# Top-32 attention and a GELU block on one core: item 0's softmax ahead of item 3's score copies, and dummies ahead of the third pair's keys

## The chip, the cores and the metric

The kernel runs on one core of a Trainium2 chip. The metric is the device time of one execution in microseconds (us). Six names are used as the profile has them: PE is TensorE (matmuls; PEld is its load of the stationary operand), DVE is VectorE, ACT is ScalarE, POOL is GpSimd, SP is SyncE, which here only issues DMAs. Every engine works through its own queue in the order in which the kernel issued the instructions; an instruction that waits holds up all that stand behind it on the same engine. "L371" is line 371 of the kernel.

## The reference

Attention over 8 batches of 8 heads, 576 positions, head size 64, in which every query keeps only its 32 largest scores; its output, laid out as 4608 tokens of 512 numbers, goes through two matrix products with an exact GELU between them. All in float32.

```python
scores = scale * np.matmul(q, k.transpose(0, 1, 3, 2))
kth = np.partition(scores, -top_k, axis=-1)[..., -top_k:-top_k + 1]
scores = np.where(scores >= kth, scores, -1000000000.0)
attn = np.exp(scores - np.max(scores, axis=-1, keepdims=True))
attn = attn / (np.sum(attn, axis=-1, keepdims=True) + 1e-09)
x = np.matmul(attn, v)   # then as (4608, 512)
h = x @ w_in
out = (0.5 * h * (1.0 + erf(h / sqrt(2)))) @ w_out
```

## The kernel before

**Items and slots.** Two heads form a pair. An item is a block of 128 queries of one pair (or the last 64 queries of two pairs), and there are 144 of them. The program is one loop over slots (`for n in range(ahead)`), and each slot holds steps of several items, written out by hand: the scores of item n+2 (`scores`), the top 32 of item n (`top_k`), the softmax of item n-1 (`select`, `softmax`), the transposes of the softmax of item n-2 (`transposes`), the product with the values for item n-3 (`attend`). From slot 10 (`START`) on, PE's remaining room goes to the two products of the GELU block (`mlp`); before that there are no tokens for it yet.

**What one item costs on each engine.** PE makes the scores: the last keys into a small PSUM tile `t_ps` (L334) and the first 512 keys of both heads into `s_ps` (L371). ACT copies them to the tile `s` in SBUF (L342 and L379; item 0's first block has a DVE copy at L339). DVE finds the 32 largest (`larger` L407, MAX8 L466, MATCH_REPLACE8 L469) with POOL helping (`sum_up` L432, `smaller` L440). POOL then makes two numbers for each row, `neg` (L480) and `bias` (L481), in `threshold`. ACT makes the softmax of each head in place in two passes: `select` pushes the scores under the threshold far down (L500), `softmax` takes the exponential and its sum `den` (L512). POOL adds 1e-9 to `den` (L493), DVE takes the reciprocal `rden` (L487), and for the first items POOL turns it into a diagonal matrix `diag` (L526), which PE uses in the transposes (L556, L590). The reciprocal of item n-1 is issued at the end of the top 32 of item n (`last`, which is `inverse(n - 1)`), so DVE waits there for ACT's softmax of item n-1.

**Keys and queries.** PE transposes the keys and queries of a pair when they have come in (L282), in three pieces: the keys, the tails of both, the queries. ACT copies each piece out of PSUM (L287). Pair 2, the third pair, has its first piece in slot 0 and the other two in slot 1 (`first`), and items 4 and 5 need them.

**Weights.** In each slot ACT takes a piece of the GELU block's weights through three passes (`weights_size`, L206, L212, L213), and POOL adds the result up (`weights_add`, L228). They are loaded by SP (L189).

**Dummies.** `keep_busy(count, m)` issues matmuls whose result nobody reads, into a PSUM tile of their own (`warm`, L1040). Each dummy shows as two records in the trace. Slots 0 to 9 each have some.

**The order around the change.** In slot 0 ACT has the copies of item 2's scores, three passes over weights and the copy of the third pair's keys. In slot 1 ACT has, in this order: the copies of item 3's scores, select and softmax of item 0, the two copies of the third pair's other pieces, three passes over weights. PE in slot 0 has the scores of item 2, the transposes of the third pair's keys, 4 dummies; in slot 1 the scores of item 3, the other transposes of the third pair, 20 dummies.

Of the kernel before, what the change touches and what calls it, by code (L numbers as in the profile page):

```python
# [14 lines left out]
def kernel(  # L15
# [51 lines left out]
    ident = const.tile([P, P], f32, name="ident")  # L67
# [80 lines left out]
    START = 2 * NP + 2  # L148
# [46 lines left out]
    def parts(u):  # L195

        t, dst = words[u], weights_of(u)[3].bitcast(i32)
        return t[:, :, 0::2], t.bitcast(mybir.dt.int16)[:, :, 2::4], t[:, :, 1::2], dst

    def weights_size(u):  # L200


        if u not in words:
            return
        w, first, below, d = parts(u)
        nc.scalar.activation(below, first, func=AF.Prelu, bias=high, scale=2.0**-40, alpha=2.0**40)  # L206
        if on_dve(u):
            nc.vector.tensor_scalar(
                w.bitcast(i32), w.bitcast(u32), 2.0**-13, None, op0=ALU.mult
            )  # L210
        else:
            nc.scalar.activation(w.bitcast(i32), w.bitcast(u32), func=AF.Copy, scale=2.0**-13)  # L212
        nc.scalar.activation(d, below, func=AF.Prelu, bias=low, scale=2.0**59, alpha=2.0**-40)  # L213

    def on_dve(u):

        return SLOT_OF[u] in ON_DVE

    def waits(u):

        return u == ORDER[-1]
# [3 lines left out]
    def weights_add(u):  # L225
        if u in words:
            w, _, _, d = parts(u)
            nc.gpsimd.tensor_tensor(d, d, w.bitcast(i32), op=ALU.add)  # L228
        made.add(u)
# [80 lines left out]
    def row(i, e):  # L310
        return S_of[i][:, e * S : (e + 1) * S]
# [14 lines left out]
    def pair_tile(name, tag="pr"):  # L326
        return ps.tile([P, 2, 512], f32, tag=tag, bufs=1, name=name)
# [76 lines left out]
    def larger(i):  # L404

        if paired(i):
            nc.vector.tensor_tensor(lists_of[i][:, :, 0], *halves_of(i), op=ALU.max)  # L407
# [28 lines left out]
    def smaller(i):  # L436

        if paired(i):
            both, top = lists_of[i][:, :, 1].bitcast(i32), lists_of[i][:, :, 0].bitcast(i32)
            nc.gpsimd.tensor_tensor(into_of(i)[:, :, 1].bitcast(i32), both, top, op=ALU.subtract)  # L440
# [42 lines left out]
    def inverse(i):  # L483
        if i < 0 or i >= N:
            return
        st = stat_of[i]
        nc.vector.reciprocal(st["rden"], st["den"])  # L487

    def add_small(i):
        if i < 0 or i >= N:  # L490
            return
        st = stat_of[i]
        nc.gpsimd.tensor_scalar(st["den"], st["den"], 1e-9, None, op0=ALU.add)  # L493

    def select(i, e):

        if i < 0 or i >= N:
            return
        st, s = stat_of[i], row(i, e)
        nc.scalar.activation(s, s, func=AF.Prelu, bias=st["neg"][:, e : e + 1], scale=1.0, alpha=STEEP)  # L500
        selected.add((i, e))
# [3 lines left out]
    def softmax(i, e):  # L505

        if i < 0 or i >= N:
            return
        st, s = stat_of[i], row(i, e)
        if (i, e) not in selected:  # L510
            select(i, e)
        nc.scalar.activation(  # L512
            s, s, func=AF.Exp, bias=st["bias"][:, e : e + 1], scale=1.0,
            accum_out=st["den"][:, e : e + 1],
        )
# [99 lines left out]
    def closes(i):  # L615

        if not few[0] or i < 0 or i >= N:
            return False
        pair, t = items[i]
        return t < NM and t % 2 == 1 and pair % NP == NP - 1  # L620

    def copy_x():
        while copies:
            copies.pop()()
# [353 lines left out]
    def run_gelus():  # L978
        while waiting:
            gelus(waiting.pop(0))  # L980
            if eager[0]:
                run_small(9)

    def run_small(room):

        while summing:
            sums(summing.pop(0))
            room -= 4
        while small and room > 0:
            n, f = small.pop(0)  # L990
            f()
            room -= n
# [11 lines left out]
    def mlp(n):  # L1004
        for _ in range(n):
            if done[0] >= len(pieces) or pieces[done[0]][0] > ready[0] or left[0] == 0:
                return
            pieces[done[0]][1]()
            done[0] += 1
            left[0] -= 1  # L1010
            if eager[0]:
                run_gelus()
                run_small(9)
# [4 lines left out]
    def room_in(n):  # L1018

        x = n - START - 1  # L1020
        if x < 1:
            return 4
        if x >= len(sizes):
            return 0
        return sizes[x] + (1 if x % 2 == 0 else -1)
# [11 lines left out]
    def keep_busy(count, m):  # L1037
        warm = pair_tile("warm", "l1")
        for _ in range(count):
            nc.tensor.matmul(warm[:, 0, 0:P], lhsT=m, rhs=m, start=True, stop=True)  # L1040
# [40 lines left out]
    for n in range(ahead):  # L1081

        left[0] = room_in(n)
        few[0] = n > START + 2
        eager[0] = n > N
        left[0] += closes(n - 3) - closes(n - 2)
        if not waits(unit_in(n)):
            weights_add(unit_in(n))
        if n > 0:
            larger(n + 1)  # L1090
        for piece in squares_in.pop(n, []):
            piece()
        two = few[0] and n % 2 == 0 and n + 3 < N and items[n + 3][1] < NM
        scores(n + 2, two)
        if two:
            scores(n + 3)
        product = attend(n - 3)
        late = n > START
        if n < START:

            for e in range(2):
                select(n - 1, e)
            softmax(n - 1, 0)
        copy_x()
        if n == START:

            for e in range(2):
                select(n - 1, e)
            softmax(n - 1, 0)
        if waits(unit_in(n)):  # L1110
            weights_size(unit_in(n))
            weights_add(unit_in(n))
        mlp(1)
        if closes(n - 3):
            ready[0] = n_tok[0]
        if few[0] and n % 2:
            run_gelus()
        tr = transposes(n - 2)
        if product and n > START and done[0] < len(pieces) and pieces[done[0]][0] > ready[0]:

            for piece in tr[:1]:
                piece(n + 2 if few[0] else None)
            tr, ready[0] = tr[1:], n_tok[0]
        if not few[0] and n > START:
            softmax(n - 1, 0)
        mlp(1)
        if not late:
            softmax(n - 1, 1)
        if few[0]:
            softmax(n - 1, 0)  # L1130
            if n % 2:
                mlp(ODD)
        mlp(1)
        prep = prep_in.pop(n, [])
        if n == 0:
            weights_size(unit_in(1))
        if n == START + 1:

            for piece in prep:
                piece(None)  # L1140
            prep = []
        if len(prep) > 1 and len(tr) == 3:
            tr, prep = tr[:1] + prep[:1] + tr[1:], prep[1:]
        now = tr[:-1]
        if few[0]:
            now, tr, prep = tr + prep[:1], [], prep[1:]
        for x, piece in enumerate(now):
            piece(n + 2 if few[0] else None)
            ready[0] = n_tok[0]
            if few[0] and x == 2:  # L1150
                break
            mlp(1)
        ready[0] = n_tok[0]
        if late:
            softmax(n - 1, 1)
        if n > 0:
            smaller(n + 1)
        add_small(n - 1)
        for piece in tr[-1:] + prep:
            piece(None)  # L1160
            mlp(1)
        if n < START:

            keep_busy(4 if n == 0 else 8 if product else 20 if n == 1 else 14 if n < 5 else 18, ident)

        run_gelus()
        mlp(left[0])
        run_gelus()
        if n < N:
            top_k(n, lambda: inverse(n - 1))  # L1170
            if n == 0:
                larger(1)
        else:
            inverse(n - 1)
        threshold(n)
        if n == 0:
            smaller(1)
        normalise(n - 1)
        sum_up(n + 2)
        if n in sums_in:  # L1180
            weight_sums(sums_in[n])
        run_small(6)

        if n > 0 and not waits(unit_in(n + 1)):
            weights_size(unit_in(n + 1))
        for m in (n + 1, n + 2):

            if m > 2 and waits(unit_in(m)) == (m == n + 1):
                load_weights(m)
        if n < NP:  # L1190
            load("v", n)
        if n == 5:
            load("q", SQUARES)
            load("k", SQUARES)
# [38 lines left out]
```

## Time and profile before

| | |
|---|---|
| median of 3 runs | 1526.88 us (1526.75 to 1527.65) |
| the profiled execution, own time | 1526.42 us |
| its span in the trace | 1524.5 us |
| PE busy in the span | 1507.2 us |
| DVE busy | 1235.8 us |
| ACT busy | 1156.2 us |
| POOL busy | 1137.7 us |
| granted TensorE clock, mean | 0.997 of full speed |

The execution's own time is 1.92 us above the span, which runs from the first to the last instruction that the trace holds. In a timeline row the first number is the start, the second the time from the start of the row's first instruction to the end of its last, then engine, line, operation, output and inputs, shape and count; brackets give the idle time before it and what ended that. The busy time of PE includes the dummies.

### The profile page before, as it was taken

Reading aid. Unit: us, or ns where it says so; the run is one execution under the profiler, and the core shown is the slowest. Engines: PE = TensorE matmul, PEld = TensorE weight load, DVE = VectorE, ACT = ScalarE, POOL = GpSimd, SP = SyncE. Lnnn points to the kernel's source line nnn. Section 1 sums busy time; section 2 is a strip of 40 time slices with the busy share of each in tenths; the row PEclk is TensorE's granted clock in tenths of the full one; section 3 lists DMA queues with packets and bytes.
Section 4 is the critical chain, followed back from the end, with each engine's and each line's share of the span. In section 5 each row is a group of like instructions: output and inputs, shape, how many; then the busy total and the mean of one; then the engine's idle time right before and its main releaser. Section 6 shows DMA issues by size and latency. Waiting matters only on the chain.

```text
span 1524.5 us, 26920 instructions
## 1 busy us (share of the span) xinstructions
PE 1507.2 (99%) x9233; PEld 1191.5 (78%) x9233; DVE 1235.8 (81%) x3270; ACT 1156.2 (76%) x2038; POOL 1137.7 (75%) x1291
## 2 busy tenths in 40 slices
PE   7999999999999999999999999999999999999999
PEld 5776677877877778888887778887787777888887
DVE  7999899988888878788888887888888887887701
ACT  6999877877778787877777778787777878787730
POOL 6777567867888868777798878786788886877742
PEclk9999999999999999999999999999999999999999
DMA  6524310111101110012201111011110111000000
GB/s 179 152 83 122 80 45 1 27 35 32 24 21 26 40 38 15 1 30 47 40 15 24 28 27 46 1 27 35 32 25 22 24 31 32 15 1 15 8 14 14
DMA packets 195016, 56.27 MB, mean 37 GB/s; under 512 B 185888, under 2 KB 186432, under 8 KB 194880
## 3 DMA queue, kind: packets, MB, share of 16 engines
q1 hardware_dynamic: 193616, 54.14, 15.1%
q8 instruction: 72, 1.18, 0.3%
q14 instruction: 64, 0.52, 0.1%
q10 hardware_dynamic: 1200, 0.39, 0.1%
q0 software_dynamic: 64, 0.03, 0.0%
HBM read 45.08 MB, written 9.44 MB: 36 GB/s over the span
## 4 chain that ended last, share of the span: by engine, by line
PE 93%; ACT 0%; DVE 0%; issue 0%; POOL 0%; DVEq 0%
PE h_ps L712 34%; PE y_ps L856 20%; PE o L654 9%; PE tp L592 8%; PE s_ps L371 7%; PE seven L854 3%; PE y_ps L818 2%; PE y_ps L800 2%; PE y_ps L821 2%; PE tp_t L334 2%; PE o L665 1%; PE s_ps L386 1%; PE tp_t L562 1%; PE tp_t L348 0%; PE warm L1040 0%; PE tp L590 0%
## 5 line engine op out<-in xcount | busy, mean ns | idle before, releaser
L712 PE MATMUL h_ps<-xT,w_in_sb 128*128 128x256 f32 (+1 forms) x2560 | 544.0, 361 | 0.1
L712 PEld LDWEIGHTS h_ps<-xT,w_in_sb 128*128 128x128 f32 x2560 | 433.7, 191 | 71.0 <-issue 25.2
L466 DVE MAX8 top<-lists 128x8 f32<-128x576 f32 (+1 forms) x792 | 477.0, 641 | 0.1
L469 DVE MATCH_REPLACE8 lists<-top,lists 128x288 f32<-128x288 f32 (+1 forms) x528 | 307.3, 587 | 0.0
L535 POOL TENSOR_TENSOR s<-s,rden 128x1152 f32<-128x1152 f32 x135 | 286.0, 2119 | 0.3 <-DVE rden L487 0.3
L493 POOL TENSOR_SCALAR den<-den 128x2 f32<-128x2 f32 x144 | 31.6, 219 | 284.5 <-ACT s L512 282.8
L512 ACT ACTIVATE s<-s,bias 128x576 f32<-128x576 f32 x288 | 224.8, 784 | 10.7
L500 ACT ACTIVATE s<-s,neg 128x576 f32<-128x576 f32 x288 | 225.8, 792 | 0.0
L606 ACT COPY pt<-tp 128x1024 f32<-128x1024 f32 x133 | 135.2, 1017 | 110.8 <-PE tp L592 110.8
L487 DVE RECIPROCAL rden<-den 128x2 f32<-128x2 f32 x144 | 23.8, 165 | 213.8 <-POOL den L493 213.3
L440 POOL TENSOR_TENSOR lists<-lists 128x576 int32<-128x576 int32 x132 | 186.4, 1412 | 4.0
L432 POOL TENSOR_TENSOR lists<-s 128x576 int32<-128x576 int32 x133 | 187.3, 1408 | 0.0
L654 PEld LDWEIGHTS o<-pt,raw_v 128*64 128x64 f32 x1280 | 87.1, 136 | 85.2 <-issue 44.3
L654 PE MATMUL o<-pt,raw_v 128*64 128x256 f32 x1280 | 153.0, 384 | 0.7 <-ACT pt L597 0.4
L856 PE MATMUL y_ps<-w_out_sb,sum 128*128 128x256 f32 x472 | 140.4, 379 | 0.0
L592 PE MATMUL tp<-ident,s 128*128 128x128 f32 x1080 | 140.1, 273 | 0.0
L592 PEld LDWEIGHTS tp<-ident,s 128*128 128x128 f32 x1080 | 126.4, 141 | 14.5 <-issue 1.9
L379 ACT ACTIVATE s<-s_ps 128x1024 f32<-128x1024 f32 x127 | 125.2, 1032 | 11.3 <-PE s_ps L371 11.2
L371 PE MATMUL s_ps<-kt,qm 64*128 64x512 f32 x512 | 130.3, 622 | 0.8 <-ACT s L377 0.8
L469 DVE MATCH_REPLACE8 lists<-first,lists 128x288 f32<-128x288 f32 x264 | 114.1, 437 | 0.0
L856 PE MATMUL y_ps<-w_out_sb,g 128*128 128x256 f32 x480 | 113.4, 379 | 0.0
L728 ACT ACTIVATE g<-h_ps 128x512 f32<-128x512 f32 x144 | 78.2, 595 | 42.1 <-PE h_ps L712 41.4
(163 smaller groups left out, 2515.1 us busy)
## 6 DMA issues: line engine op xcount, KB each, us to landing
raw_v<-in_v_dram SPq DMA_DIRECT2D x64, 128.0 KB, 2.3
out_dram<-y SPq DMA_DIRECT2D x30, 256.0 KB, 2.0
raw_q<-in_q_dram SPq DMA_DIRECT2D x112, 64.0 KB, 2.0
raw_k<-in_k_dram SPq DMA_DIRECT2D x112, 64.0 KB, 2.0
w_out_sb<-in_moe_w_in_dram SPq DMA_DIRECT2D x14, 511.8 KB, 4.7
w_out_sb<-in_moe_w_out_dram SPq DMA_DIRECT2D x10, 511.8 KB, 4.3
w_sum<-in_moe_w_out_dram SPq DMA_DIRECT2D x6, 511.8 KB, 4.3
raw_q<-in_q_dram SPq DMA_DIRECT2D x112, 8.0 KB, 1.8
```

The lines of the kernel that those rows point to most:

```text
L371: nc.tensor.matmul(s_ps[:, e], lhsT=q_t[rows, :], rhs=kt[rows, 0:SM], start=True, stop=True)
L432: nc.gpsimd.tensor_tensor(t[:, :, 1].bitcast(i32), a.bitcast(i32), b.bitcast(i32), op=ALU.add)
L440: nc.gpsimd.tensor_tensor(into_of(i)[:, :, 1].bitcast(i32), both, top, op=ALU.subtract)
L466: nc.vector.max(x[:, e], src[:, e])
L469: nc.vector.match_replace(dst[:, e], x[:, e], src[:, e], LOWEST)
L500: nc.scalar.activation(s, s, func=AF.Prelu, bias=st["neg"][:, e : e + 1], scale=1.0, alpha=STEEP)
L512: nc.scalar.activation(s, s, func=AF.Exp, bias=st["bias"][:, e : e + 1], scale=1.0, accum_out=st["den"][:, e : e + 1],)
L535: nc.gpsimd.tensor_tensor(s, s, wide, op=ALU.mult)
L592: nc.tensor.transpose(to, part, ident)
L654: nc.tensor.matmul(o[e * D : (e + 1) * D, 0:n], lhsT=vt[:, j, e, :], rhs=pt[:, e * NM + j if j < NM else 2 * NM, :], start=(j == 0), stop= ...
L712: nc.tensor.matmul(h_tile(u)[:, i, :], lhsT=w_in_sb[:, ko, f * P : (f + 1) * P], rhs=xT[:, ko, c0 : c0 + n], start=(ko == 0), stop=(ko == ...
L856: nc.tensor.matmul(acc[names][:, k], lhsT=lhsT, rhs=rhs, start=(j == 0 and k == 0), stop=(j == FT // 2 - 1 and k == 1),)
```

## The change

Three edits. In slot 1 the select and the softmax of item 0, both heads, are issued ahead of `scores(3)`, where they stood behind it; the two old places skip slot 1. In slot 0 there are 14 new dummies, issued behind `weights_size` and ahead of the transposes of the third pair's keys. In slot 1 the dummies at the end go from 20 to 14.

```diff
+        if n == 1:
+
+            for e in range(2):
+                select(0, e)
+            for e in range(2):
+                softmax(0, e)
         two = few[0] and n % 2 == 0 and n + 3 < N and items[n + 3][1] < NM
         scores(n + 2, two)
...
-        if n < START:
+        if n != 1 and n < START:
 
             for e in range(2):
                 select(n - 1, e)
...
-        if not late:
+        if n != 1 and not late:
             softmax(n - 1, 1)
...
         if n == 0:
             weights_size(unit_in(1))
+            keep_busy(14, ident)
...
-            keep_busy(4 if n == 0 else 8 if product else 20 if n == 1 else 14 if n < 5 else 18, ident)
+            keep_busy(4 if n == 0 else 8 if product else 14 if n < 5 else 18, ident)
```

## The prediction

> **What bounds the kernel now.** I read the windows of the whole span first, cut where the busy shares change. The columns are the window, its length, then busy time and instructions of PE, PEld, DVE, ACT and POOL, then the granted TensorE clock, the DMA share and GB/s.
>
> ```profile
> 18.00:24.00 6.00, 5.29 (x19) 3.59 (x20) 6.00 (x19) 2.57 (x5) 5.88 (x5) 0.50 0.56 126
> 24.00:30.00 6.00, 6.00 (x50) 5.88 (x52) 4.41 (x11) 6.00 (x11) 4.02 (x7) 0.93 0.68 195
> 30.00:105.00 75.00, 69.72 (x548) 57.10 (x547) 71.00 (x193) 75.00 (x131) 59.34 (x59) 1.00 0.43 133
> 105.00:1524.50 1419.50, 1415.17 (x8565) 1117.39 (x8563) 1143.95 (x3018) 1064.34 (x1885) 1061.78 (x1207) 1.00 0.13 29
> ```
>
> There are three stages. From 105 us on PE is busy for 1415.17 of 1419.50 us: that stage has its own length, and whatever happens ahead of it can only move its start. From 30 to 105 us ACT is busy for 75.00 of 75.00 us, while PE's 69.72 include dummies and DVE has 4 us free: ACT sets the pace of slots 2 to 9. From 18 to 24 us ACT is busy for 2.57 us only, and PE's clock is at half speed. So the question is what holds ACT between 18 and 24 us. The waits of ACT in the window 17 to 105 us, and those of DVE in the window 17 to 107 us, are these (who waited for whom, sum, times, longest):
>
> ```profile
> ACT s L379 <- PE s_ps L371: 1.7, 1, 1.7
> ACT s L342 <- PE t_ps L334: 1.5, 1, 1.5
> ```
> ```profile
> DVE rden L487 <- POOL den L493: 6.1, 9, 1.6
> ```
>
> ACT's list is complete: after the second of its waits it never waits again before 105 us. DVE's one kind of wait, nine times, is for the sum that ACT's softmax makes. So in this stage ACT leads and DVE follows. The timeline of ACT shows where the two waits stand:
>
> ```profile
> 18.45 1.24 ACT L213 ACTIVATE w_in_sb<-w_out_sb,low 128x1024 int32<-128x1024 f32 x1
> 19.83 0.59 ACT L287 COPY kt<-tp_qk 128x512 f32<-128x512 f32 x1
> 21.97 0.28 ACT L342 ACTIVATE s<-t_ps 128x128 f32<-128x128 f32 x1 [1.55 <-PE t_ps L334]
> 23.99 1.02 ACT L379 ACTIVATE s<-s_ps 128x1024 f32<-128x1024 f32 x1 [1.74 <-PE s_ps L371]
> 24.91 1.43 ACT L500 ACTIVATE s<-s,neg 128x576 f32<-128x576 f32 x2
> ...
> 27.76 0.35 ACT L287 COPY kt<-tp_qk 128x256 f32<-128x256 f32 x1
> 28.01 0.58 ACT L287 COPY qm<-tp_qk 128x512 f32<-128x512 f32 x1
> 28.49 1.26 ACT L206 ACTIVATE w_out_sb<-w_out_sb,high 128x1024 f32<-128x1024 int16 x1
> ...
> 30.70 1.24 ACT L213 ACTIVATE w_in_sb<-w_out_sb,low 128x1024 int32<-128x1024 f32 x1
> 31.83 0.27 ACT L342 ACTIVATE s<-t_ps 128x128 f32<-128x128 f32 x1
> 31.98 1.02 ACT L379 ACTIVATE s<-s_ps 128x1024 f32<-128x1024 f32 x1
> ```
>
> Both waits are for the scores of item 3, which PE makes at half clock. The softmax of item 0 stands behind them, though its inputs come from POOL and DVE. PE and POOL in the same stretch:
>
> ```profile
> 14.24 1.13 PE L371 MATMUL s_ps<-kt,qm 64*128 64x512 f32 x4
> 18.71 1.09 PE L282 MATMUL tp_qk<-ident,raw_k 128*128 128x128 f32 x4 [3.34 <-DMA raw_k<-in_k_dram]
> 19.59 1.91 PE L1040 MATMUL warm<-ident 128*128 128x128 f32 x8
> ...
> 21.86 2.08 PE L371 MATMUL s_ps<-kt,qm 64*128 64x512 f32 x4
> ...
> 25.01 4.63 PE L1040 MATMUL warm<-ident 128*128 128x128 f32 x40
> ...
> 36.05 0.44 PE L282 MATMUL tp_qk<-ident,w_sum 128*128 128x128 f32 x2 [2.39 <-ACT pt L572]
> ```
> ```profile
> 18.12 1.31 POOL L480 TENSOR_SCALAR neg<-top 128x2 f32<-128x2 f32 x1 [3.00 <-DVE top L466]
> ...
> 24.64 1.40 POOL L440 TENSOR_TENSOR lists<-lists 128x576 int32<-128x576 int32 x1
> ...
> 29.05 0.61 POOL L526 TENSOR_TENSOR diag<-ident,rden 128x256 f32<-128x256 f32 x1
> ```
>
> PE stands idle for 3.34 us until the third pair's keys land at 18.71. After that the same four records of `s_ps` take 2.08 us, not the 1.13 of item 2, and a dummy takes 1.91/4 = 0.48 us, not 4.63/20 = 0.23.
>
> **The change part by part.** *The softmax moved ahead.* Nothing is added on ACT: two selects and two exponentials with their sums, 27.76 - 24.91 = 2.85 us, go from behind the two waits to ahead of them. What they need is there: `neg` is done at 18.12 + 1.31 = 19.43, and `bias`, a short step next on POOL, follows. ACT gets to them after the copy of the keys at about 20.1. Their cover was the wait itself: 1.55 + 1.74 = 3.29 us of listed idle time, a little more than 2.85. No DMA goes with them, and no queue of SP or POOL is passed. Behind them on ACT now stand the copies of item 3's scores; who waits for those is DVE's `larger` of item 3, which in its queue comes after the reciprocal of item 0, at 26.6 at the earliest.
>
> *The 14 dummies in slot 0.* They take 14 x 0.23 = 3.2 us and start when item 2's scores are through, at 15.4, so they end at about 18.6, just under the landing of the keys at 18.71. Their cover is the 3.34 us wait, and they cost nothing as long as they run at full clock. What they should do is keep the clock: then the key transposes take about 1.09/2 = 0.55 us and end at 19.3, the 4 dummies behind them end at 20.2, and item 3's scores (0.4 and 1.13 us) are done at 21.8, two microseconds before 23.94. The six transposes of the third pair's other pieces, 0.14 us each at full clock, are done at 22.6.
>
> *20 to 14 dummies in slot 1.* They end at 22.6 + 3.2 = 25.8, and item 4's scores (1.5 us) at 27.3. ACT will ask for them at 28.2 (below), so they cost nothing; six more (1.4 us) would end at 28.7 and cost half a microsecond.
>
> *The sum on ACT.* I count start to start, since instructions overlap a little. The weights pass at 18.45 lets the next start after 1.13 us (30.70, the same pass, to 31.83 in slot 2), so ACT is free at 19.58 and the keys are there at 19.3. Then: key copy 0.48 (as 28.01 to 28.49, the same shape), softmax 2.85, small score copy 0.15 (31.83 to 31.98), large one 0.92 (23.99 to 24.91), the copies of the other pieces 28.49 - 27.76 = 0.73. Together 5.13, so the next weights pass starts at 19.58 + 5.13 = 24.71 and not at 28.49: **3.78 us earlier**. By the listed idle times alone it would be 3.29; the difference is the overlap and 0.25 us of waiting ahead of the key copy. Item 3's scores (21.8) are there before ACT asks (22.9), the other pieces (22.6) before 24.0. Those are the two ends, 3.29 and 3.78, and I take 3.78, since start to start is how ACT paces slots 2 to 9.
>
> *What is late next.* The lead has to survive until 105 us. DVE's own room is this:
>
> ```profile
> 28.19 0.17 DVE L487 RECIPROCAL rden<-den 128x2 f32<-128x2 f32 x1 [1.59 <-POOL den L493]
> ...
> 36.21 0.15 DVE L487 RECIPROCAL rden<-den 128x2 f32<-128x2 f32 x1
> ...
> 45.30 0.17 DVE L487 RECIPROCAL rden<-den 128x2 f32<-128x2 f32 x1 [0.96 <-POOL den L493]
> ...
> 54.43 0.17 DVE L487 RECIPROCAL rden<-den 128x2 f32<-128x2 f32 x1 [1.04 <-POOL den L493]
> ...
> 105.53 0.17 DVE L487 RECIPROCAL rden<-den 128x2 f32<-128x2 f32 x1 [0.57 <-POOL den L493]
> ```
>
> The reciprocal of item 0 can come 1.59 us earlier; POOL's step before it can run when the row at 24.64 ends, at 26.04, just in time. At item 1 DVE has no wait to give, so it stays 1.59 ahead; at item 2 the room is 2.55, at item 3 it is 3.59, and the whole list has 6.1. So DVE is the late one for two slots, and from item 4 on ACT leads again with all of its 3.78.
>
> The timeline of slot 2 and the page's line on the weights' loads (us from issue to landing at its end) give the other two checks:
>
> ```profile
> 25.19 1.06 SPq L189 DMA_DIRECT2D w_sum<-in_moe_w_in_dram  x2
> ...
> 35.74 0.26 ACT L572 COPY pt<-tp_t 128x128 f32<-128x128 f32 x1
> ...
> 37.58 1.32 ACT L206 ACTIVATE w_sum<-w_sum,high 128x1024 f32<-128x1024 int16 x1
> ```
> ```profile
> w_out_sb<-in_moe_w_in_dram SPq DMA_DIRECT2D x14, 511.8 KB, 4.7
> ```
>
> Does ACT feel DVE in those two slots? It needs DVE for the diagonal matrix: item 0's stood at 29.66 and comes 1.6 earlier, at about 28.0; PE then needs under 3 us for its transposes (it waited 2.39 us for ACT at 36.05 after them), and ACT copies the first of them at 35.74 - 3.78 = 31.96. That holds with about 1 us to spare. The weights that slot 2 takes up were issued at 25.19 to 26.25 and land 4.7 later, at about 31; ACT asks for them at 37.58 - 3.78 = 33.8. Later loads wait for steps of POOL or DVE that move forward too. So the stage that starts at 105 us starts 3.78 earlier and keeps its 1419.5 us, since everything in it waits for something in it.
>
> The profiled execution's own time, 1526.42, would become 1522.64. It lies 0.46 under the median of the runs, so for a median I take 1526.88 - 3.78 = **1523.1 us**.
>
> *One rule against the row.* PE's gap of 3.34 us ended at half clock; the gap of 2.39 us ahead of 36.05 left the clock at 1.00. So the length at which the clock falls lies between, and the longest gap that I expect after the change, 1.5 us in slot 2, is under both. The Trainium skill, page "TensorE: Matmul & The Clock Gate", section "What's actually happening", puts the fall after at least one idle window of about 3.4 us; the row shows a slightly shorter gap that already sufficed. By the letter of the page the gap alone would not explain the fall, the clock could fall with the dummies too, and the sum would be that of the first rival; the trace, with 1.00 behind 2.39 us and 0.50 behind 3.34, speaks for the gap.
>
> **The rivals.** *The clock falls all the same* at about 18 us (the stretch before it had PE idle too, in short pieces). Then the scores of item 3 stay at 23.94, ACT copies them at 23.99 and reaches the weights at about 25.7, 2.8 ahead; but item 4's scores, behind 14 dummies that start at 25.2, end at 29.7, and the copy comes at 29.75, not at 31.98: 2.2 us gained, **1524.7**. Against it: the dummies fill the only long gap.
>
> *DVE or POOL sets the pace*: the diagonal matrices, which move by 1.59 only, hold PE's transposes and with them ACT's copies. Then 1.6 us gained, **1525.3**. For it: DVE has no slack at item 1. Against it: the 1 us to spare worked out above, and DVE's waits at items 2 and 3.
>
> *The lead is given back*, by a DMA or a buffer that the trace of before does not show as late, somewhere before 105 us: **1526.9**. Against it: ACT waits for no such thing in 75 us.
>
> *Slower: the new dummies run at half clock* and stand ahead of the keys in PE's queue. Then they take 14 x 0.48 = 6.7 us, to 22.1, the keys are through at 23.2, item 3's scores at 27.7, the other pieces at 29.2; with 14 full-speed dummies item 4's scores come at 33.9, where ACT copied them at 31.98: 1.9 lost, **1528.8**. If those 14 run at half clock too, it is 38.5, and 6.5 lost, 1533.4. It decides from the point where the dummies end later than the keys land by more than ACT's 0.3 us of room there, that is above about 0.25 us each. Against it: item 2's scores right before them run at full clock (1.13).
>
> **How the numbers follow.** The forecast with its 3.29 to 3.78 has 0.70; the clock that falls 0.09, DVE or POOL 0.08, the lead given back 0.05, slower dummies 0.08, a little over half of it in the dear form. 0.2% is 3.05 us, about what a measurement of this kernel can tell from no change; that is 1523.83 and 1529.93. The forecast lies beyond it by 0.2 to 0.7 us, all three cases in the middle and the cheap half of the slower one lie inside. So faster 0.70, same 0.25, slower 0.05. The range goes from 1522.3 (3.78, and the 0.46 that the profiled execution lay under the median, and a little more) to 1525.3 (DVE or POOL), which leaves out the last two cases, 0.13, and some of the edges.
>
> **What would show it.** Right: in the windows of the changed kernel the clock in 18 to 24 us is 1.00; `s_ps` of item 3 takes 1.13 us and ends near 21.8; ACT has L500 and L512 of item 0 between 20.1 and 22.9 and no wait over 0.3 us; L206 of slot 1 starts near 24.7; DVE's waits for `den` are gone at items 0 to 2 and nearly at item 3; the reciprocal that stood at 105.53 stands near 101.8. Wrong: dummies of slot 0 that end after 19 us, a clock of 0.50 in that window, an ACT wait for the tiles `tp` or `tp_t` in slot 2, or a lead that is 3.8 at 25 us and less at 100.

## The result, and the profile after

The changed kernel takes 1522.61 us (median of 9 runs, 1522.4 to 1523.12), the kernel before in 9 runs beside it 1527.2 (1526.46 to 1528.05): a ratio of 0.9971, 95% interval 0.996 to 0.9981, 4.6 us. The forecast was 1523.1. The span of the profiled execution goes from 1524.5 to 1520.8 us, 3.7 less. Of all executions behind this document one ran in a slow state, one of the seven with four dummies (2982.5 us at a mean clock of 0.881), and it is left out of the range given there.

The windows of the changed kernel, cut as for the kernel before but with the last border 3.7 us earlier (length; busy time and instructions of PE, PEld, DVE, ACT, POOL; granted clock, DMA share, GB/s):

```profile
18.00:24.00 6.00, 6.00 (x48) 4.96 (x48) 6.00 (x19) 6.00 (x11) 5.71 (x5) 1.00 0.46 102
24.00:30.00 6.00, 4.54 (x37) 3.42 (x36) 6.00 (x17) 6.00 (x10) 5.61 (x8) 1.00 0.74 198
30.00:101.30 71.30, 66.99 (x531) 54.66 (x530) 69.37 (x187) 71.30 (x126) 58.12 (x58) 1.00 0.47 142
101.30:1520.80 1419.50, 1415.21 (x8565) 1117.43 (x8563) 1143.94 (x3018) 1063.76 (x1885) 1060.90 (x1207) 1.00 0.13 29
```

ACT is busy for 6.00 of the 6 us from 18 to 24, where it had 2.57, and the clock there is 1.00, not 0.50. The last stage is the same stage: 1419.5 us, PE 1415.21 busy, the same 8565 records. ACT's timeline shows what fills the hole:

```profile
18.69 1.26 ACT L213 ACTIVATE w_in_sb<-w_out_sb,low 128x1024 int32<-128x1024 f32 x1
19.84 0.57 ACT L287 COPY kt<-tp_qk 128x512 f32<-128x512 f32 x1
20.30 1.45 ACT L500 ACTIVATE s<-s,neg 128x576 f32<-128x576 f32 x2
...
23.16 0.27 ACT L342 ACTIVATE s<-t_ps 128x128 f32<-128x128 f32 x1
23.32 1.02 ACT L379 ACTIVATE s<-s_ps 128x1024 f32<-128x1024 f32 x1
24.22 0.37 ACT L287 COPY kt<-tp_qk 128x256 f32<-128x256 f32 x1
24.48 0.60 ACT L287 COPY qm<-tp_qk 128x512 f32<-128x512 f32 x1
24.95 1.28 ACT L206 ACTIVATE w_out_sb<-w_out_sb,high 128x1024 f32<-128x1024 int16 x1
```

No row has an idle time, and ACT's next wait comes at 103.40 us only. The softmax of item 0 runs from 20.30 to 23.16, the score copies follow at once, and the weights pass of slot 1 starts at 24.95. PE and the reciprocals on DVE:

```profile
15.48 3.39 PE L1040 MATMUL warm<-ident 128*128 128x128 f32 x28
18.86 0.63 PE L282 MATMUL tp_qk<-ident,raw_k 128*128 128x128 f32 x4
...
20.54 1.13 PE L371 MATMUL s_ps<-kt,qm 64*128 64x512 f32 x4
...
28.34 0.44 PE L556 MATMUL tp_t<-diag,s 128*64 128x128 f32 x4 [1.46 <-POOL diag L526]
...
32.48 0.44 PE L282 MATMUL tp_qk<-ident,w_sum 128*128 128x128 f32 x2 [1.33 <-ACT pt L572]
```
```profile
26.68 0.15 DVE L487 RECIPROCAL rden<-den 128x2 f32<-128x2 f32 x1
34.65 0.15 DVE L487 RECIPROCAL rden<-den 128x2 f32<-128x2 f32 x1
42.70 0.15 DVE L487 RECIPROCAL rden<-den 128x2 f32<-128x2 f32 x1
50.85 0.17 DVE L487 RECIPROCAL rden<-den 128x2 f32<-128x2 f32 x1
59.21 0.17 DVE L487 RECIPROCAL rden<-den 128x2 f32<-128x2 f32 x1 [0.28 <-POOL den L493]
...
101.86 0.17 DVE L487 RECIPROCAL rden<-den 128x2 f32<-128x2 f32 x1 [0.56 <-POOL den L493]
```

The 14 dummies run at full clock and fill the gap; item 3's scores take 1.13 us; DVE's waits at items 0 to 3 are gone (1.59, none, 0.96 and 1.04 us before) and from item 4 on they are back at their old size. The tenth reciprocal comes at 101.86 where it came at 105.53: 3.67 us.

That tenth reciprocal is a good mark for all that follows. In the twelve traces of the two kernels and of all the experiments below, what lies behind it has one length to 0.3 us, so only its place matters:

| kernel | tenth reciprocal, us | span, us | span behind it |
|---|---|---|---|
| before (the profile of the prediction) | 105.53 | 1524.5 | 1419.0 |
| before, two other executions | 106.55, 106.44 | 1525.5, 1525.4 | 1419.0, 1419.0 |
| changed | 101.86 | 1520.8 | 1418.9 |
| order alone | 102.34 | 1521.3 | 1419.0 |
| dummies alone | 103.31 | 1522.2 | 1418.9 |
| 28 dummies in slot 0 | 104.98 | 1523.9 | 1418.9 |
| 4 dummies in slot 0 | 102.17 | 1521.1 | 1418.9 |
| 20 dummies in slot 1 | 102.00 | 1521.0 | 1419.0 |
| one weights pass on DVE | 100.71 | 1519.9 | 1419.2 |
| slot 2's gap filled, else as before | 104.90 | 1523.8 | 1418.9 |
| one weights pass on DVE, gap filled | 101.18 | 1520.3 | 1419.1 |

### The profile page after: what moved, and what is told of

The parts are those of the page before. It is cut to its first block, busy times and chain, and to the rows that moved or that the text cites. A ratio compares the mean times of both kernels' runs of the same rounds, so it can differ in the third digit from the quotient of the medians.

```text
span 1520.8 us, 26952 instructions
## 1 busy us (share of the span) xinstructions
PE 1506.9 (99%) x9249; PEld 1191.2 (78%) x9249; DVE 1235.6 (81%) x3270; ACT 1155.1 (76%) x2038; POOL 1137.0 (75%) x1291
## 4 chain that ended last, share of the span: by engine, by line
PE 94%; ACT 0%; DVE 0%; issue 0%; POOL 0%; DVEq 0%
PE h_ps L712 34%; PE y_ps L856 20%; PE o L654 9%; PE tp L592 8%; PE s_ps L371 7%; PE seven L854 3%; PE y_ps L818 2%; PE y_ps L800 2%; PE y_ps L821 2%; PE tp_t L334 2%; PE o L665 1%; PE s_ps L386 1%; PE tp_t L562 1%; PE tp_t L348 0%; PE warm L1040 0%; PE tp L590 0%
```

## The experiments

My theory was the prediction's: ACT sets the pace from slot 1 to slot 9, so the time moves by what ACT no longer waits in slot 1; the order and the clock each take a part of that wait. The rivals: the order is all of it, the clock is all of it, or DVE and POOL become the bound. The experiments were run in three groups on three chips; beside them the kernel before took 1527.38, 1527.61 and 1527.14 us, against 1527.2 above. So differences of a few tenths between medians of different groups mean little.

**The order alone**: the changed kernel without the new dummies.

```diff
             weights_size(unit_in(1))
-            keep_busy(14, ident)
```

> The changed kernel without the 14 dummies in slot 0 (softmax of item 0 ahead, 14 dummies in slot 1). My theory: the order alone lets ACT fill the wait, but PE goes to half clock in the gap ahead of the keys, so item 3's scores end near 24 us and, behind them, item 4's scores near 29.7 to 30; ACT's copy of item 4's large score block starts near 29.8 and not at 28.4, so about 2.2 us less than the kernel before, 1.5 more than the changed one: 1524.1 to 1525.0. Rival one, the order is the whole of it: 3.7 less than before, same as the changed kernel, with the clock at 0.50 in 18 to 24 us. Rival two, the clock is the whole of it: same as before.

Measured: 1523.36 us (10 runs, 1522.94 to 1524.26), 0.9975 of the kernel before (0.9965 to 0.9984), so 4.0 us less and 0.75 above the changed kernel (0.5 by the marks). I had expected 1.5 above, 1524.1 to 1525.0, and missed. PE's row shows why:

```profile
22.08 1.34 PE L371 MATMUL s_ps<-kt,qm 64*128 64x512 f32 x4
```

The clock fell here too, but it came back during item 3's scores, which took 1.34 and not 2.08 us and were done at 23.4, about when ACT has finished the softmax. So the order is most of the gain; in this trace the half clock ended at 22.56 us, 2.2 us sooner than in the profile of before, and left the dummies less to save.

**The dummies alone**: the kernel before with 14 dummies in slot 0 and 14 at the end of slot 1.

> The kernel before, its order kept, with 14 dummies in slot 0 and 14 in slot 1. My theory: the clock stays at 1.00, item 3's scores end at 21.7 instead of 23.9, ACT still waits for them about 1.2 us with the softmax behind; slot 1's first weights pass starts near 26.3 and not at 28.5 (lead 2.2 us), so about 2.2 us less than before: 1524.1 to 1525.0. Rival one, the order is the whole of it: same as before. Rival two, the clock is the whole of it: 3.7 less, same as the changed kernel.

Measured: 1525.4 us (11 runs, 1524.02 to 1526.65), 0.9988 (0.9979 to 0.9997): 2.0 less, and 0.4 above the upper end of what I expected. In its trace the mark stands 2.2 us earlier than in the profile of before, as worked out, with the weights pass at 26.28. Neither rival fits: the two parts overlap (4.0 and 2.0 alone, 4.6 to 4.8 together; by the marks 3.2, 2.2 and 3.7), because both take from the same wait. The spread of 2.6 us was not expected. The profiled execution is one of the two fastest: these two have a mean clock of 1.000 and took 1524.0 and 1524.2, the other nine have 0.998 or 0.999 and took 1525.1 to 1526.7. So a fall of the clock in the other executions, as found below in the kernel before, is the likely reason; no trace of one was kept.

**Twice the dummies**: 28 in slot 0.

> The changed kernel with 28 dummies in slot 0 and not 14. My theory: PE's queue is in order, so the key transposes start near 22.1 and not at 18.9; ACT copies the keys near 22.7, 2.9 us later, and the softmax of item 0 stands behind that copy; ACT's lead falls from 3.7 to about 0.8 us: about 1525.5, 2.9 above the changed kernel. Rival: ACT has room and PE's lateness is taken up again by the end of slot 1, under 1 us lost.

Measured: 1525.8 us (11 runs, 1525.47 to 1526.62), 0.9991 (0.9982 to 0.9999): 3.2 above the changed kernel, 2.9 expected.

```profile
15.88 6.52 PE L1040 MATMUL warm<-ident 128*128 128x128 f32 x56
22.24 0.60 PE L282 MATMUL tp_qk<-ident,raw_k 128*128 128x128 f32 x4
```
```profile
22.88 0.59 ACT L287 COPY kt<-tp_qk 128x512 f32<-128x512 f32 x1 [2.54 <-PE tp_qk L282]
```

This is how the prediction's "slower" rival would cost time: the keys stand behind the dummies, ACT waits 2.54 us for them, and the softmax cannot pass that copy in ACT's queue.

**Four dummies in slot 0**, not 14.

> The changed kernel with 4 dummies in slot 0 and not 14: PE is idle from about 16.4 to 18.9, 2.4 us. My theory: the clock falls by the length of the gap, 3.3 us was enough and 2.4 was not, so the clock stays at 1.00 and the time is that of the changed kernel within 0.2 us. Rival, the share of busy time in a fixed window decides: the clock falls to 0.50 and the run is like the order alone, about 1.5 us slower than the changed kernel.

Measured: 1522.93 us (median of 7 runs; six lie between 1522.86 and 1522.97), 0.9971 (0.996 to 0.9983): 0.3 above the changed kernel. The time is what I expected, and the reason is not. The clock did fall, for 3.4 us, at 18.4, some 2.1 us into a gap of 2.68 us:

```profile
18.94 1.09 PE L282 MATMUL tp_qk<-ident,raw_k 128*128 128x128 f32 x4 [2.68 <-DMA raw_k<-in_k_dram]
```
```profile
18.00:19.00 1.00, 0.06 (x1) 0.09 (x2) 1.00 (x2) 1.00 (x2) 1.00 (x1) 0.70 0.43 95
19.00:21.00 2.00, 2.00 (x10) 2.00 (x11) 2.00 (x8) 1.41 (x3) 2.00 (x4) 0.50 0.52 116
21.00:22.00 1.00, 1.00 (x8) 0.88 (x7) 1.00 (x6) 1.00 (x3) 1.00 (x1) 0.59 0.67 151
```

Some 2.1 us idle were enough here, and 2.39 were not in the profile of before: so a gap's length alone does not decide, against my theory. The rival's rule, the share of busy time in a fixed window, had the clock right and the time wrong: the run cost 0.3 us and not 1.5, because ACT was busy with the softmax until the clock was back.

**The kernel before, twice more.** The medians gave more (4.6) than the two profiles (3.7).

> The kernel before, unchanged, in another execution. The changed kernel gained 4.6 us by the medians and 3.7 by the two profiled executions. My theory: the stretch at half clock has another length in each execution, and the profile of before on which the prediction rests had a short one (18.0 to 24.4 us); a longer one delays item 3's scores further, ACT's second wait grows by as much, and the span with it: an execution near 1527.5 us shows half clock for 9 us or more, or a later end of it, and slot 1's first weights pass later than 28.5 by what the time is above 1526.4. Rival: the trace ahead of 30 us is the same, and the missing 0.9 us lies in the stage after 105 us.

> The kernel before a second time, as the run ahead of this: my theory says that time and the start of slot 1's first weights pass move together between executions, one for one, and that the stage after the tenth reciprocal keeps its 1419 us; the rival says that the start does not move.

Measured: 1527.44 and 1527.33 us. Both the theory and its rival fall. The first stretch at half clock was not longer, the weights pass of slot 1 not later but earlier (28.05 and 28.02, not 28.49), and the last stage the same; still the mark came 1.0 and 0.9 later. The loss lies in slot 2. The windows of the first of these executions, then PE's rows:

```profile
15.00:16.00 1.00, 0.22 (x2) 0.00 (x0) 1.00 (x5) 0.73 (x1) 0.00 (x0) 0.91 1.04 341
16.00:22.00 6.00, 3.01 (x14) 2.95 (x14) 6.00 (x17) 4.12 (x5) 4.04 (x4) 0.50 0.77 157
22.00:23.00 1.00, 1.00 (x5) 0.51 (x4) 1.00 (x3) 0.28 (x1) 1.00 (x2) 0.68 0.69 155
23.00:36.00 13.00, 10.25 (x84) 8.59 (x81) 11.69 (x32) 12.45 (x23) 9.98 (x11) 1.00 0.54 140
36.00:37.00 1.00, 1.00 (x9) 1.00 (x7) 1.00 (x3) 1.00 (x4) 1.00 (x3) 0.65 0.94 270
37.00:39.00 2.00, 2.00 (x11) 2.00 (x11) 2.00 (x10) 2.00 (x4) 1.82 (x2) 0.50 1.01 361
39.00:40.00 1.00, 1.00 (x8) 1.00 (x8) 1.00 (x4) 1.00 (x2) 0.00 (x0) 0.65 1.34 322
```
```profile
35.61 0.44 PE L282 MATMUL tp_qk<-ident,w_sum 128*128 128x128 f32 x2 [2.75 <-ACT pt L572]
35.88 4.92 PE L1040 MATMUL warm<-ident 128*128 128x128 f32 x28
40.64 0.39 PE L334 MATMUL t_ps<-kt,qm 128*128 128x128 f32 x2
```
```profile
41.06 0.28 ACT L342 ACTIVATE s<-t_ps 128x128 f32<-128x128 f32 x1 [0.49 <-PE t_ps L334]
42.13 1.03 ACT L379 ACTIVATE s<-s_ps 128x1024 f32<-128x1024 f32 x1 [0.79 <-PE s_ps L371]
```

The clock fell a second time, at 36.3, after PE's wait for ACT in slot 2. The 14 dummies of that slot took 4.92 and not 3.29 us, item 5's scores came late, and ACT waited 0.49 + 0.79 = 1.28 us for them. In the profile on which the prediction rests the same gap (2.39 us) passed without a fall.

**That gap filled**: the kernel before, with 10 dummies more where PE waits in slot 2.

```diff
-        for piece in tr[-1:] + prep:
+        for x, piece in enumerate(tr[-1:] + prep):
             piece(None)
             mlp(1)
+            if n == 2 and x == 0:
+                keep_busy(10, ident)
```

> The kernel before, and 10 dummies more in slot 2, between PE's transposes of item 0 and the tails of the fourth pair's keys, where PE waits 2.4 to 2.75 us for ACT. In two executions of the kernel before the clock fell a second time there, at 36.4 us, and ACT waited 1.3 us for item 5's scores; in the one that the prediction rests on it did not. My theory: this second fall is the 0.9 us by which the medians exceed the prediction; with the gap filled it cannot happen, and the kernel takes 1526.4 in all of its executions, 1.0 below the median of the kernel before. Rival: the gap is not what makes the clock fall, or the dummies delay the tails: same as before, 1526.4 to 1528.

Measured: 1526.1 us (11 runs, 1525.5 to 1526.85) beside 1527.14 for the kernel before on the same chip (15 runs, 1526.33 to 1527.87), 0.9994 (0.9985 to 1.0003): 1.0 less, as worked out, though the interval takes in 1; its slowest execution is still below the median beside it, and its trace has the clock at 1.00 from 23 to 40 us. The times spread over 1.3 us and are not one value, which I had expected: the first fall is left and has its own length, 3.4 us at half clock in this profile and 6.8 in the one of before. How often the second fall comes these traces cannot say. That its removal gives the 1.0 us back is what the medians say, to the width of that interval.

**20 dummies in slot 1**, as before the change.

> The changed kernel with 20 dummies at the end of slot 1 and not 14. My theory: they end at 26.9, item 4's large score block at 28.3, where ACT asks for it at 28.4, so nothing or up to 0.3 us is lost: 1522.6 to 1523.0. Rival: the cut from 20 to 14 was needed, half a microsecond or more lost (the prediction's figure): 1523.1 or above.

Measured: 1522.83 us (7 runs, 1522.72 to 1523.06), 0.9971 (0.996 to 0.9982): 0.2 above the changed kernel, too little to tell apart. In the trace item 4's scores end at 28.39 and ACT's large copy starts at 28.44, 0.26 after the small one where 0.15 is usual: a tenth of a microsecond. The third edit is next to nothing by itself.

**One weights pass on DVE.** What is left is ACT's own work, so the second pass of the weights of slot 2 goes to DVE, which has 2.5 us of waits left.

```diff
-        else:
+        elif u != unit_in(2):
             nc.scalar.activation(w.bitcast(i32), w.bitcast(u32), func=AF.Copy, scale=2.0**-13)
...
+        if n == 2:
+            larger(n + 1)
+            w = parts(unit_in(2))[0]
+            nc.vector.tensor_scalar(w.bitcast(i32), w.bitcast(u32), 2.0**-13, None, op0=ALU.mult)
         if not waits(unit_in(n)):
             weights_add(unit_in(n))
-        if n > 0:
+        if n > 0 and n != 2:
             larger(n + 1)
```

> The changed kernel, and the second of the three weights passes that ACT makes at the end of slot 1 goes to DVE, behind larger of item 3 in slot 2. My theory: ACT still sets the pace to 100 us, so taking 1.06 us of its work away moves the tenth reciprocal from 101.9 to 100.8; DVE takes 0.73 us more, against 2.5 us of waits that it has left. 1521.3 to 1521.8, about 1.0 below the changed kernel. Rival: after the change DVE and POOL are the bound in slots 1 to 3, and 0.7 us more on DVE gives nothing or makes it slower: 1522.6 to 1523.3.

Measured: 1521.86 us (7 runs, 1521.66 to 1523.46), 0.9968 (0.9957 to 0.9979). The mark moves to 100.71, 1.15 earlier, and DVE's waits shrink to three at the end of the stage: ACT is still the bound there, while at the six items ahead of them DVE has no wait left to give. It beats both kernels by its median, but two of the seven executions took 1523.4, at a mean clock of 0.999.

**The same with PE's gap in slot 2 filled** (6 dummies behind item 4's scores).

```diff
+        if n == 2:
+            keep_busy(6, ident)
         product = attend(n - 3)
```

> The version with one weights pass on DVE, and 6 dummies more in slot 2 between item 4's scores and item 0's transposes, where PE waits 1.6 us for the diagonal matrix. Two of seven executions of that version took 1523.4 at a mean clock of 0.999, the others 1521.8 at 1.000. My theory: those two had a stretch at half clock that begins in this gap, so with the gap filled all executions take 1521.6 to 1521.9. Rival: the gap is too short to matter and some executions still take 1523.4.

Measured: 1521.96 us (5 runs, 1521.53 to 1522.33), 0.9966 (0.9953 to 0.9978). None of five took 1523.4; with two of seven before, that can be chance, so where those two lost their time stays open. That all five would lie in 1521.6 to 1521.9 did not come true (they spread over 0.8 us), and the median is the same as without these dummies.

## Why the prediction was right

*What bounds the kernel.* Right, and shown by the table of marks: the last stage keeps its length to 0.3 us in twelve traces, and ACT sets the place of the mark. Taking one pass of 1.0 us off ACT and giving it to DVE moved the mark by 1.15.

*The softmax ahead, and the sum on ACT.* The weights pass was to start at 24.71 and started at 24.95, in a trace in which slot 0 already stands 0.24 us later (L213 at 18.69, not 18.45): 3.78 forecast, 28.49 - 24.95 + 0.24 = 3.78 found, 3.54 without that shift. The mark moved by 3.67.

*The dummies of slot 0.* They ended at 18.87, which is 18.6 with the later start taken off, kept the clock, and item 3's scores were done at 21.7, as forecast (21.8). What they are worth is less than the prediction's rival without them says: 0.75 us by the medians and 0.5 by the marks, in place of 1.6 (3.78 - 2.2), since the clock came back earlier than in the profile of before.

*20 to 14.* Right that it costs nothing; the half microsecond that 20 would cost was a tenth to 0.2.

*What is late next.* Right in order and size: DVE late at items 1 and 2, level at item 3, ACT leading from item 4. The diagonal matrix came early enough: PE waited 1.46 us for it and then still 1.33 us for ACT, the longest gaps left (1.5 forecast).

*The step that was mis-sized* is the last of the sum, "for a median I take 1526.88 - 3.78". It takes one execution's waits for those of all. In other executions the kernel before has a second fall of the clock, which the change removes as well: ACT asks earlier in slot 2, and PE's gap there is 1.33 us and not 2.4 to 2.75. By the medians the gain is 4.6, by the profiles 3.7; the second fall measured 0.9 and 1.0 at the mark in two executions. All nine executions of the changed kernel have a mean clock of 1.000. That 1523.1 lies only 0.5 from 1522.61 is in part luck: the gain came out 0.8 larger than 3.78, and the median of the kernel before 0.3 higher than the 1526.88 from which it was taken.

*The step that was wrong* is "the length at which the clock falls lies between" 2.39 and 3.34 us. A gap of 2.68 and one of 2.75 were followed by half clock, one of 2.39 was not; that alone would leave room for a border between 2.39 and 2.68. But with the dummies alone the gap in slot 2 was 2.75 us long too (31.08 to 33.83), and there the clock stayed at 1.00:

```profile
30.00:36.00 6.00, 3.25 (x29) 3.06 (x28) 6.00 (x15) 6.00 (x13) 5.11 (x6) 1.00 0.59 164
```

The same length, and both outcomes. In the row of windows of the first other execution above the clock is at half from 15.82 (0.91 in the first microsecond is 0.18 us at half) to 22.64, and from 36.30 to 39.70: 6.8 and 3.4 us, and 13.66 between the end of the one and the start of the other, which is four times 3.4. In the run with four dummies it is 18.40 to 21.82, 3.4 again. So the clock changes at the marks of a grid of 3.4 us. The profile of before gives its own grid in two rows:

```profile
17.00:18.00 1.00, 0.00 (x0) 0.00 (x0) 1.00 (x3) 1.00 (x2) 0.00 (x0) 0.99 1.03 166
...
24.00:25.00 1.00, 1.00 (x6) 1.00 (x7) 1.00 (x3) 1.00 (x2) 1.00 (x2) 0.60 0.08 6
```

Half clock from 17.98 to 24.8, again 6.8, so the marks lie at 31.6, 35.0 and 38.5, and the gap from 33.67 to 36.05 is cut at 35.0; in the other execution it lay whole (32.85 to 35.61) between 32.9 and 36.3.

How much of one gap lies between two marks is not all that counts, either: the fall at 15.82 comes only 0.6 us after PE went idle. PE's busy time between two marks, all short gaps included, sorts the cases. I cut the six traces that have a fall into windows at their own marks; the table has the falls ahead of 105 us and the four least busy windows without one (the second other execution repeats the first):

| trace | between the marks, us | PE busy of 3.41 us | clock after |
|---|---|---|---|
| slot 2's gap filled | 15.35 to 18.76 | 0.00 | half |
| before, first other execution | 32.88 to 36.30 | 0.69 | half |
| before | 14.57 to 17.98 | 0.80 | half |
| four dummies in slot 0 | 14.99 to 18.40 | 1.27 | half |
| before, first other execution | 12.41 to 15.82 | 1.69 | half |
| order alone | 12.31 to 15.72 | 1.80 | half |
| before | 4.33 to 7.74 | 1.96 | full |
| order alone | 29.37 to 32.78 | 2.01 | full |
| before | 31.63 to 35.05 | 2.04 | full |
| slot 2's gap filled | 11.93 to 15.35 | 2.07 | full |

Up to 1.80 us (53%) the clock was lost, and from 1.96 us (57%) on it was kept, in every window of these six traces that began at full clock. The traces without a fall ahead of 105 us have their grid from the one behind PE's last work, counted back in steps of 3.4133 us (worked out in the last section). With the dummies alone (fall at 1520.80) it cuts the gap in slot 2 at 32.59, with 1.91 and 2.17 us busy on its two sides. With one pass on DVE (fall at 1520.26) the window from 25.22 to 28.63, which has PE's gap of 1.61 us, is busy for 1.80 us and kept the clock; so the border lies near 1.8 us, and the two executions of 1523.4 us may have lost their time there, which is not shown. The gaps of 1.46 and 1.33 us that the changed kernel has left lie too far apart to fall whole between the same two marks, so at worst 3.41 - 1.46 = 1.95 us are busy: the forecast that they are harmless held, with less room than its rule by length suggested.

The Trainium skill, page "TensorE: Matmul & The Clock Gate", section "What's actually happening", calls the window 3413 ns long and free-running, not starting with the kernel; the traces agree with both. They differ from its idle window: the one from 32.88 to 36.30 had PE busy for 0.69 us, the one from 12.31 to 15.72 with the order alone for 1.80 us, and the clock fell all the same. In the prediction I used that section for the length only, and passed over that the grid lies differently in each execution.

## What to carry to other kernels

When an engine that sets the pace waits in its own queue, look for work behind the wait whose inputs are ready: moving it ahead hid nearly all of a late producer here (4.0 us, where both parts together gave 4.6 to 4.8), while making the producer faster gave 2.0, and the two overlap. A gain at the start is carried to the end whole if the stage that follows is bound by another engine with a fixed length; one instruction near the border, here the tenth reciprocal, then tells to a tenth of a microsecond where one execution stands, though executions of one kernel can differ by more (105.53, 106.55 and 106.44 us here). One profile shows one position of the clock's grid: where PE's gaps add up to about half of 3.4 us, profile a second execution before the sum is made.

## What the runs showed of the hardware that I had not expected

The stretches at half clock last 3.4 or 6.8 us and begin and end on a grid of 3.4 us that lies elsewhere in each execution. The grid runs on to the end: in the first other execution of the kernel before the clock falls once more behind PE's last work, at 1524.50 us, 1508.68 after the first fall, or 442 times 3.4133. As far as these traces go, the clock is lost by the busy share of a whole window, with the border near 1.8 of 3.41 us, and not by the length of one gap. After the first fall of the profile of before PE was at work again from 18.71, and the clock was back only at 24.8; after the fall in the run with four dummies it worked from 18.94 and had its clock back at 21.8. So 2.7 us of work in a window of 3.4 left the clock at half, and 2.9 us brought it back; what the share must be on the way back, and whether transposes count in it as other matmuls do, these runs do not tell.
